# An FFT and two gated layers on one core: decoding the weights in place a pair ahead, with other first turns

## The chip, the cores and the metric

The kernel runs on one NeuronCore of a Trainium2 chip. The metric is the device time of one execution in microseconds. Before the change it is 1013.66 us, the median of three runs (1013.66 to 1013.98).

## What is computed

The input `x` is (2, 3008, 256) in float32. The reference takes the real part of its two-dimensional FFT over sequence and feature, and passes the 6016 rows through two layers whose weights are given in float64:

```python
X = np.fft.fft(np.fft.fft(x, axis=1), axis=2).real.astype(np.float32)
h = X @ w_in                       # 256 -> 2048
X = (h * sigmoid(h)) @ w_out       # 2048 -> 256
h = X @ w_in2
out = (h * np.clip(h + 3, 0, 6) / 6) @ w_out2
```

## The kernel before

**FFT.** `step1`, `step2` and `step3` are three stages of small matmuls; the first comes in 11 chunks of x (`XCH`), the others in 12 steps `g` (`steps23`). `evacuate` copies the result of `step3` from PSUM into `eo`. The symmetry of the transform lets layer one work on 3010 pairs of rows, in six `CHUNKS` of 502 (the last has 500).

**Units.** Each layer is cut into units `(k, f)`: `k` is a turn (`segs`: a chunk and a range of `f`), `f` a block of 128 (layer one) or 256 (layer two) of the 2048 hidden features. Layer one has 96 units in 12 turns: each chunk has a first turn of `PARTS[j]` blocks and, after all six, a second turn with the rest. So the last weights are needed late. Layer two has 96 units as well; its first four turns take blocks 0 to 3, the next four blocks 4 to 7.

A product in float32 accuracy is three matmuls (`mm3`): both operands are split into a rounded part (`hi`) and the rest (`lo`). A unit of layer one runs on PE as `win1` (6 matmuls into `ab`), on DVE as three instructions that make `h`, on ACT as two Silu activations (`parts`, into `ghi` and in place), on POOL as the subtraction `glo` (`low`), and three units later (`LAG`) as `wout1` (12 matmuls into `y`). `ab` and `h` have two buffers each, so `win1` of a unit waits for the `h` of the unit two before it, and that `h` for the `glo` two before. At a turn's end `y` is copied (first turn, ACT) or added (second turn, DVE, L555) to `y1`.

**Weights.** They lie in HBM as pairs of 32-bit words, in eight pairs of blocks per layer. A pair `g` goes through `load_raw` (1 MB by SP's queue), `magnitude` (ACT, L98), five instructions of `bits_to_float32` (DVE, L104 to L116), the additions of `finish_w1` (DVE, L168 to L174), or of `finish_w2`, and `divide`: `whi` on ACT (L161), then `wlo` on DVE (L163). `decoder` is a generator that yields a cost after each DVE instruction; `advance` runs it for a credit in ns, and a PAUSE ends the turn of `advance`. `spare` gives the credit, once per unit in layer one. `win1` drives the generator on where a unit's weights are not yet issued. Four pairs of layer two (`STAGED`) are decoded in layer one's second turns, stored to HBM, and loaded and split shortly before layer two; the other four are decoded in layer two.

**Order.** The program's order is the order on each engine (a manual schedule): nothing is reordered later. The first two units (`EARLY`) are issued at g = 12 and 13, behind the last steps of the FFT.

Of the kernel before, what the change touches and what calls it, by code (L numbers as in the profile page):

```python
# [36 lines left out]
F32 = mybir.dt.float32  # L37
F32R = mybir.dt.float32r
# [21 lines left out]
XCH += [(1, 0, 3), (1, 3, 4), (1, 7, 4), (1, 11, 4), (1, 15, 2)]  # L60
QA = NA + 1

PARTS = (4, 4, 6, 8, 10, 12)
TURNS = 4
LAG = 3
EARLY = 2
# [4 lines left out]
def body(tc, xh, x128, t1, t2, t3, w1, w128, w2, out):  # L71
    nc = tc.nc
    V, A, T, G = nc.vector, nc.scalar, nc.tensor, nc.gpsimd
    per = tc.alloc_tile_pool(name="per", bufs=1)
    wp = tc.alloc_tile_pool(name="wp", bufs=8)
    dp = tc.alloc_tile_pool(name="dp", bufs=1)
    dr = tc.alloc_tile_pool(name="dr", bufs=1, space=bass.MemoryType.DRAM)
    eop = tc.alloc_tile_pool(name="eop", bufs=1, side="right")

# [7 lines left out]

    whi, wlo, raws = {}, {}, {}

    def load_raw(key, src, g, pool=dp):  # L90
        raws[key, g] = pool.tile([P, 2, 512, 2], U32, name=f"raw_{key}_{g}", tag="raw")
        nc.sync.dma_start(raws[key, g], src[:, 2 * g : 2 * g + 2, :, :])


# [2 lines left out]
    def magnitude(raw, t):  # L97
        A.activation(t, raw[..., 1].bitcast(F32), AF.Abs)  # L98

    def bits_to_float32(raw, t, a):  # L100

        high, ai, ti = raw[..., 1].bitcast(I32), a.bitcast(I32), t.bitcast(I32)

        V.tensor_scalar(out=t, in0=t, scalar1=2.0**-15, scalar2=None, op0=ALU.max)  # L104
        yield 680
        V.tensor_scalar(
            out=ai, in0=ti, scalar1=3, scalar2=0x3FFFFFFF, op0=ALU.logical_shift_left, op1=ALU.bitwise_and
        )
        yield 680
        V.scalar_tensor_tensor(  # L110
            out=ai, in0=high, scalar=-0x40000000, in1=ai, op0=ALU.bitwise_and, op1=ALU.bitwise_or
        )
        yield 1200
        V.tensor_scalar(out=ti, in0=ai, scalar1=-0x800000, scalar2=None, op0=ALU.bitwise_and)
        yield 680
        V.scalar_tensor_tensor(out=t, in0=raw[..., 0], scalar=2.0**-52, in1=t, op0=ALU.mult, op1=ALU.mult)  # L116
        yield 1200

    def decoder(key, src, finish, first=0, end=NF // 2, pools=()):

        for g in range(first, end):
            if g >= first + len(pools):
                load_raw(key, src, g)
                yield PAUSE
            a = dp.tile([P, 2, 512], F32, name="da", tag="da")
            raw = raws.pop((key, g))
            if g < first + len(pools):
                if g == first:
                    ts = [q.tile([P, 2, 512], F32, name="dt", tag="dt") for q in pools]
                    magnitude(raw, ts[0])  # L130
                    yield PAUSE
                t = ts[g - first]
            else:
                t = dp.tile([P, 2, 512], F32, name="dt", tag="dt")
                magnitude(raw, t)
                yield PAUSE
            yield from bits_to_float32(raw, t, a)
            if g + 1 < first + len(pools):
                magnitude(raws[key, g + 1], ts[g + 1 - first])
            yield from finish(g, t, a)  # L140
# [12 lines left out]
    def weight_tiles(key, g):
        whi[key, g] = wp.tile([P, 2, 512], F32R, name=f"whi{key}_{g}", tag="whi")
        wlo[key, g] = wp.tile([P, 2, 512], F32R, name=f"wlo{key}_{g}", tag="wlo")

    finished = []

    def divide(key, g, t):
        hi, lo = whi[key, g], wlo[key, g]  # L160
        A.activation(hi, t, AF.Copy)  # L161
        yield PAUSE
        finished.extend([V.tensor_tensor(out=lo, in0=t, in1=hi, op=ALU.subtract)] * 2)  # L163
        yield 1200

    def finish_w1(g, t, a):
        weight_tiles(1, g)
        V.tensor_tensor(out=a[:, :, 0:256], in0=a[:, :, 0:256], in1=t[:, :, 0:256], op=ALU.add)  # L168
        yield 680
        V.tensor_tensor(out=t[:, :, 256:512], in0=a[:, :, 256:512], in1=t[:, :, 256:512], op=ALU.add)  # L170
        yield 680
        V.tensor_tensor(out=t[:, :, 0:128], in0=a[:, :, 0:128], in1=a[:, :, 128:256], op=ALU.add)
        yield 420
        V.scalar_tensor_tensor(  # L174
            out=t[:, :, 128:256], in0=a[:, :, 0:128], scalar=mask, in1=a[:, :, 128:256],
            op0=ALU.mult, op1=ALU.subtract,
        )
        yield 420
        yield from divide(1, g, t)

    def finish_w2(g, t, a):
        weight_tiles(2, g)
        V.tensor_tensor(out=t, in0=a, in1=t, op=ALU.add)
        yield 1200
        yield from divide(2, g, t)

    def store_w2(g, t, a):
        V.tensor_tensor(out=t, in0=a, in1=t, op=ALU.add)
        nc.sync.dma_start(w2_d[g], t)
        yield 1200  # L190

    def load_w2(g):
        raws[g] = dp.tile([P, 2, 512], F32, name=f"w2_{g}", tag="raw")
# [4 lines left out]
        split(whi[2, g], wlo[2, g], raws.pop(g))  # L198

    def decode_w128(raw):  # L200
        t, a = (dp.tile([P, NF], F32, name=n, tag=n) for n in ("w128t", "w128a"))
        magnitude(raw, t)
        yield PAUSE
        for _ in bits_to_float32(raw, t, a):
            yield 70
        V.tensor_tensor(out=w128_sb, in0=a, in1=t, op=ALU.add)
        yield 70
# [144 lines left out]
    steps = itertools.chain(
        decode_w128(w128_raw), decoder(1, w1, finish_w1, pools=(fft, dp)), decoder(2, w2, store_w2, 0, STAGED)
    )
    steps2 = decoder(2, w2, finish_w2, STAGED)
# [5 lines left out]
    def step1_next():  # L361

        nonlocal folded, i
        x = folded
        if i + 4 < nx:
            load_x(i + 4)
        if i + 1 < nx:
            folded = fold(i + 1)
        step1(i, x)
        i += 1  # L370
        if i == 1:
            nc.sync.dma_start(t2_sb, t2)
            nc.sync.dma_start(t3_sb, t3)
            nc.sync.dma_start(w128_raw, w128)
        if i < 5:
            busy(3)
        if i == 5:
            step1_last()
        if i == nx - 4:
            load_raw(1, w1, 0, fft)  # L380
            load_raw(1, w1, 1)
            advance(steps, 1)
        if i == nx - 3:
            advance(steps, 400)

    def steps23(g):
        nonlocal done
        if g < 12:
            o2[g] = step2(g)
        if 0 <= g - 1 < 12:  # L390
            full[g - 1] = step3(o2.pop(g - 1))
        if 0 <= g - 2 < 12:
            done = evacuate(g - 2, full.pop(g - 2))

    while XCH[i][0] == 0:
        step1_next()
    while i < nx:
        steps23(g)
        g += 1
        step1_next()  # L400
        do_later()
        if i >= nx - 1:
            advance(steps, 2500 if i < nx else 1500)
    xp.release()
    psX.release()

# [74 lines left out]
    ]  # L481
    while g < 14:
        steps23(g)
        if g >= 12:
            k, f = units[g - 12]
            gs[k, f] = win1(k, f)
            parts(k, f)
        do_later()
        if g == 8:
            xs[0] = split_eo(0)  # L490
        advance(steps, 1300)
# [95 lines left out]
    for i in range(len(units) + LAG):  # L587
        if i < len(units):
            k, f = units[i]
            layer, j, fs = segs[k]  # L590
            
            if i >= EARLY:
                gs[k, f] = (win1 if layer == 1 else win2)(k, f)
        if 1 <= i <= len(units):
            low(*units[i - 1])
        if i >= LAG:
            k_, f_ = units[i - LAG]
            (wout1 if segs[k_][0] == 1 else wout2)(k_, f_)
# [12 lines left out]
        if 2 <= i < turn:
            spare()
        elif i < n1:

            if i == turn:
                for _ in steps:
                    pass
                load_w2(0)
            g, odd = divmod(i - turn, 2)
            if odd and 0 < g < STAGED:  # L620
                load_w2(g)
            elif not odd and 0 < g <= STAGED:
# [138 lines left out]
```

## Time and profile before

| | |
|---|---|
| median of three runs | 1013.66 us |
| profiled execution | 1013.63 us, span 1011.8 us |
| PE busy | 974.9 us (96%) |
| DVE / ACT / POOL busy | 664.5 (66%) / 513.0 (51%) / 237.5 us (23%) |
| mean granted clock | 0.988 |

The span runs from the first to the last instruction. Busy shares are means over stages: POOL works in layer one alone, and DVE decodes the weights there. A row of a timeline gives start, duration, engine, line, operation and tiles, and in brackets how long the engine had been idle and what released it.

### The profile page before, as it was taken

To read this page: it belongs to the slowest core of one execution; us is meant where nothing else is said; L and a number is where in the kernel's file an instruction comes from. 1 tells how busy PE (TensorE), PEld (TensorE's weight loads), DVE (VectorE), ACT (ScalarE), POOL (GpSimd) and SP (SyncE) were. 2 spreads that over 40 slices of the span, in tenths; PEclk is the share of its full clock that TensorE was granted. 3 is DMA by queue.
4 is the path that set the end of the run, shared out by engine and by line. 5 is a ranking of instruction groups with operands and counts; after the bars stand their busy time and mean duration, and the time that the engine had idled before them with its cause. 6 is when DMAs were issued, how large, how long until landed. Compare 5 with 4: busy or idle time off the path is not lost.

```text
span 1011.8 us, 10957 instructions
## 1 busy us (share of the span) xinstructions
PE 974.9 (96%) x4416; PEld 807.4 (80%) x4416; DVE 664.5 (66%) x724; ACT 513.0 (51%) x559; POOL 237.5 (23%) x101
## 2 busy tenths in 40 slices
PE   8959899999998999999999899999999999999998
PEld 7847678887777888888888688888888888888886
DVE  6769788889997888786777654554534444444443
ACT  3745566565555555565555444443444434344342
POOL 0025556565556565555000000000000000000000
PEclk9979899999999999999999999999999999999999
DMA  9311011011102111021111000000000000000000
GB/s 364 119 52 52 11 42 53 0 52 53 42 1 72 63 54 47 25 74 42 42 41 42 1 21 21 21 20 1 21 21 1 21 1 21 0 21 21 1 21 20
DMA packets 11007, 40.46 MB, mean 40 GB/s; under 512 B 1350, under 2 KB 6348, under 8 KB 8140
## 3 DMA queue, kind: packets, MB, share of 16 engines
q1 hardware_dynamic: 10812, 39.49, 10.9%
q8 instruction: 34, 0.56, 0.2%
q10 hardware_dynamic: 144, 0.27, 0.1%
q14 instruction: 17, 0.14, 0.0%
HBM read 31.48 MB, written 8.27 MB: 39 GB/s over the span
## 4 chain that ended last, share of the span: by engine, by line
PE 81%; DVE 10%; ACT 3%; issue 3%; POOL 1%; DMA 1%; ACTq 0%; POOLq 0%; DVEq 0%
PE y L231 15%; PE y L232 15%; PE y L233 15%; PE ab L233 12%; PE ab L231 12%; PE ab L232 12%; DVE h L461 2%; DVE h L464 2%; POOL glo L531 1%; DMA x<-in_xh 1%; DVE h L465 1%; DVE wlo L163 1%; DVE dt L104 1%; ACT h L475 1%; PE ps L281 1%
## 5 line engine op out<-in xcount | busy, mean ns | idle before, releaser
L231 PE MATMUL y<-ghi,whi 128*128 128x502 f32 (+1 forms) x768 | 301.1, 392 | 2.7 <-DVE y L555 2.7
L233 PE MATMUL y<-ghi,wlo 128*128 128x502 f32 (+1 forms) x768 | 300.8, 392 | 0.0
L232 PE MATMUL y<-glo,whi 128*128 128x502 f32 (+1 forms) x768 | 300.3, 391 | 0.0
L531 POOL TENSOR_TENSOR glo<-h,ghi 128x1004 fp32r<-128x1004 f32 (+1 forms) x96 | 237.1, 2471 | 237.3 <-ACT h L475 209.6
L521 DVE SCALAR_TENSOR_TENSOR h<-h,ab 128x1004 f32<-128x1004 f32 (+1 forms) x96 | 115.2, 1200 | 258.6 <-ACT h L520 258.4
L520 ACT ACTIVATE h<-ab,three 128x1004 f32<-128x1004 f32 (+1 forms) x96 | 105.5, 1099 | 159.5 <-PE ab L233 143.9
L474 ACT ACTIVATE ghi<-h 128x1004 fp32r<-128x1004 f32 (+1 forms) x96 | 100.1, 1043 | 164.3 <-DVE h L465 159.9
L231 PEld LDWEIGHTS y<-ghi,whi 128*128 128x128 f32 x768 | 145.4, 189 | 33.8 <-issue 3.1
L232 PEld LDWEIGHTS y<-glo,whi 128*128 128x128 f32 x768 | 145.9, 190 | 30.9
L233 PEld LDWEIGHTS y<-ghi,wlo 128*128 128x128 f32 x768 | 145.2, 189 | 30.4
L472 ACT ACTIVATE ghi<-h 128x1004 fp32r<-128x1004 f32 (+1 forms) x96 | 100.3, 1045 | 122.0 <-DVE h L521 122.0
L233 PE MATMUL ab<-uhi,wlo 128*128 128x502 f32 (+1 forms) x384 | 150.6, 392 | 3.7 <-DVE wlo L163 3.7
L231 PE MATMUL ab<-uhi,whi 128*128 128x502 f32 (+1 forms) x384 | 150.3, 391 | 0.0
L232 PE MATMUL ab<-ulo,whi 128*128 128x502 f32 (+1 forms) x384 | 150.1, 391 | 0.0
L531 DVE TENSOR_TENSOR glo<-h,ghi 128x1004 fp32r<-128x1004 f32 (+1 forms) x96 | 114.9, 1197 | 0.0
L461 DVE SCALAR_TENSOR_TENSOR h<-eb,w_sb,ab 128x502 f32<-128x502 f32 (+1 forms) x96 | 70.3, 732 | 52.6 <-PE ab L233 39.3
L475 ACT ACTIVATE h<-h 128x1004 f32<-128x1004 f32 (+1 forms) x96 | 100.2, 1044 | 8.7
L231 PE MATMUL ab<-xhi,whi 128*128 128x502 f32 (+1 forms) x192 | 76.5, 398 | 16.9 <-ACT whi L161 12.7
L233 PEld LDWEIGHTS ab<-uhi,wlo 128*128 128x128 f32 x384 | 72.6, 189 | 19.2 <-DVE wlo L163 4.1
L232 PEld LDWEIGHTS ab<-ulo,whi 128*128 128x128 f32 x384 | 72.8, 190 | 15.3
L231 PEld LDWEIGHTS ab<-uhi,whi 128*128 128x128 f32 x384 | 72.7, 189 | 15.2
L233 PE MATMUL ab<-xhi,wlo 128*128 128x502 f32 (+1 forms) x192 | 76.5, 398 | 3.0 <-DVE wlo L163 2.9
(76 smaller groups left out, 800.0 us busy)
## 6 DMA issues: line engine op xcount, KB each, us to landing
raw<-in_w SPq DMA_DIRECT2D x16, 1024.0 KB, 4.8
x<-in_xh SPq DMA_DIRECT2D x6, 1024.0 KB, 6.8
out<-y SPq DMA_DIRECT2D x20, 251.0 KB, 2.2
eb<-e_d SPq DMA_DIRECT2D x10, 251.0 KB, 3.3
w_d<-dt SPq DMA_DIRECT2D x4, 512.0 KB
w<-w_d SPq DMA_DIRECT2D x4, 512.0 KB, 3.2
x<-in_xh SPq DMA_DIRECT2D x3, 512.0 KB
out<-y SPq DMA_DIRECT2D x4, 250.0 KB, 2.0
```

The lines of the kernel that those rows point to most:

```text
L104: V.tensor_scalar(out=t, in0=t, scalar1=2.0**-15, scalar2=None, op0=ALU.max)
L231: T.matmul(o, wh, xhi, start=first, stop=False)
L232: T.matmul(o, wh, xlo, start=False, stop=False)
L233: T.matmul(o, wl, xhi, start=False, stop=last)
L461: V.scalar_tensor_tensor(out=h[:, 0, :n], in0=eb[:, :n], scalar=w128_sb[:, f : f + 1], in1=ab[:, 0, :n], op0=ALU.mult, op1=ALU.add)
L464: V.tensor_tensor(out=h[:, 1, :n], in0=h[:, 0, :n], in1=ab[:, 1, :n], op=ALU.subtract)
L472: A.activation(ghi[:, :, :n], h[:, :, :n], AF.Copy)
L474: A.activation(ghi[:, :, :n], h[:, :, :n], AF.Silu)
L475: A.activation(h[:, :, :n], h[:, :, :n], AF.Silu)
L520: A.activation(h[:, :, :n], hp[:, :, :n], AF.Relu, bias=three)
L521: V.scalar_tensor_tensor(out=h[:, :, :n], in0=h[:, :, :n], scalar=6.0, in1=hp[:, :, :n], op0=ALU.min, op1=ALU.mult)
L531: eng.tensor_tensor(out=glo[:, :, :n], in0=h[:, :, :n], in1=ghi[:, :, :n], op=ALU.subtract)
```

## The change

It does six things. The first turns are of 2, 4, 4, 6, 8 and 10 units. Each pair's decoding uses as scratch the place in which the next pair's weights will lie (`begin`, `scratch`; pools `wp` with a tag per pair); the scratch tiles' room becomes a second buffer for raw words (`dp` with two). `load_raw` runs two pairs ahead and the magnitude one pair ahead of the DVE work. `whi` is issued at a pair's end, and `wlo` (`last_step`) after the second instruction of the next pair. The first two units are issued at g = 11 and 12, inside the FFT, and `xs[0]` and `xs[1]` at g = 7 and 10; `evacuate` goes ahead of `step2`. `spare` gives 1150 per unit (1500 for the first four), and the pairs staged for layer two have a generator of their own (`stage`).

```diff
-PARTS = (4, 4, 6, 8, 10, 12)
+PARTS = (2, 4, 4, 6, 8, 10)
...
-    wp = tc.alloc_tile_pool(name="wp", bufs=8)
-    dp = tc.alloc_tile_pool(name="dp", bufs=1)
+    wp = tc.alloc_tile_pool(name="wp", bufs=1)
+    dp = tc.alloc_tile_pool(name="dp", bufs=2)
...
+    def begin(key, g):
+        if g + 1 < NF // 2:
+            scratch[g] = [wp.tile([P, 2, 512], F32, name=f"{n}{key}_{g}", tag=f"w{n}{g + 1}") for n in ("hi", "lo")]
+        else:
+            both = dp.tile([P, 2, 2, 512], F32, name=f"ta{key}", tag="raw")
+            scratch[g] = [both[:, 0], both[:, 1]]
+        magnitude(raws[key, g], scratch[g][1])
+
+    def decoder(key, src, add, first=0, end=NF // 2):
+        def last_step(g):
+            t = scratch.pop(g)[1]
+            finished.extend([V.tensor_tensor(out=wlo[key, g], in0=t, in1=whi[key, g], op=ALU.subtract)] * 2)
 
         for g in range(first, end):
...
+            (a, t), raw = scratch[g], raws.pop((key, g))
+            for n, cost in enumerate(bits_to_float32(raw, t, a)):
+                yield cost
+                if n == 1 and g > first:
+                    last_step(g - 1)
+                    yield 1200
+            if g + 2 < end:
+                load_raw(key, src, g + 2)
+            if g + 1 < end:
+                begin(key, g + 1)
+            yield from add(t, a)
+            weight_tiles(key, g)
+            A.activation(whi[key, g], t, AF.Copy)
+        yield PAUSE
+        last_step(end - 1)
+        yield 1200
...
+        if i + 4 == nx - 1:
+            load_raw(1, w1, 0)
...
     def steps23(g):
         nonlocal done
+        if 0 <= g - 2 < 12:
+            done = evacuate(g - 2, full.pop(g - 2))
         if g < 12:
             o2[g] = step2(g)
         if 0 <= g - 1 < 12:
             full[g - 1] = step3(o2.pop(g - 1))
-        if 0 <= g - 2 < 12:
-            done = evacuate(g - 2, full.pop(g - 2))
...
-            advance(steps, 1200 if i < 54 else 900)
+            advance(steps, 1500 if i < 4 else 1150)
...
-        if g >= 12:
-            k, f = units[g - 12]
+        do_later()
+        if g in (7, 10):
+            xs[g // 10] = split_eo(g // 10)
+        if g >= 11 and g - 11 < EARLY:
+            k, f = units[g - 11]
             gs[k, f] = win1(k, f)
             parts(k, f)
...
-            elif g > STAGED and i >= n1 - 2:
-                advance(steps2, 1)
+            elif g > STAGED:
+                if i == n1 - 4:
+                    load_raw(2, w2, STAGED)
+                    load_raw(2, w2, STAGED + 1)
+                elif i == n1 - 1:
+                    begin(2, STAGED)
```

In the orders below, `whi1_1` is layer 1, pair 1; `dt` and `da` (before) and `lo` and `hi` (after) are the scratch tiles; the h rows are three to a unit.

On DVE, from the `h` of unit 1 before the change on:

```order
L465 TENSOR_TENSOR h_567<-h_567,ab_566 128x502
L168 TENSOR_TENSOR da_511<-da_511,dt_380 128x2x256
L170 TENSOR_TENSOR dt_380<-da_511,dt_380 128x2x256
L172 TENSOR_TENSOR dt_380<-da_511 128x2x128
L174 SCALAR_TENSOR_TENSOR dt_380<-da_511,mask_73 128x2x128
L163 TENSOR_TENSOR wlo1_1_581<-dt_380,whi1_1_580 128x1024
L461 SCALAR_TENSOR_TENSOR h_606<-eb0_488,w128_sb_71,ab_605 128x502
```

and from the last decode instruction of the same pair after it, ahead of the `h` of unit 2:

```order
L180 SCALAR_TENSOR_TENSOR lo1_1_474<-hi1_1_473,mask_73 128x2x128
L471 SCALAR_TENSOR_TENSOR h_610<-eb1_532,w128_sb_71,ab_609 128x502
L474 TENSOR_TENSOR h_610<-h_610,ab_609 128x502
L475 TENSOR_TENSOR h_610<-h_610,ab_609 128x502
L104 TENSOR_SCALAR lo1_2_591<-lo1_2_591 128x1024
L106 TENSOR_SCALAR hi1_2_590<-lo1_2_591 128x1024
L471 SCALAR_TENSOR_TENSOR h_631<-eb1_532,w128_sb_71,ab_630 128x502
L474 TENSOR_TENSOR h_631<-h_631,ab_630 128x502
L475 TENSOR_TENSOR h_631<-h_631,ab_630 128x502
L142 TENSOR_TENSOR wlo1_1_626<-lo1_1_474,whi1_1_625 128x1024
L110 SCALAR_TENSOR_TENSOR hi1_2_590<-raw_1_2_471,hi1_2_590 128x1024
```

`wlo1_1` stood ahead of the `h` of unit 2; now the `h` of units 2 and 3 and the first two instructions of pair 2 stand ahead of it.

On DVE at the start of pair 6, before the change behind the `h` of unit 37:

```order
L104 TENSOR_SCALAR dt_1721<-dt_1721 128x1024
L106 TENSOR_SCALAR da_1720<-dt_1721 128x1024
L110 SCALAR_TENSOR_TENSOR da_1720<-raw_1_6_1690,da_1720 128x1024
L461 SCALAR_TENSOR_TENSOR h_1760<-eb5_1405,w128_sb_71,ab_1759 128x500
```

and after it behind the `h` of unit 28:

```order
L104 TENSOR_SCALAR lo1_6_1431<-lo1_6_1431 128x1024
L471 SCALAR_TENSOR_TENSOR h_1507<-eb5_1204,w128_sb_71,ab_1506 128x500
L474 TENSOR_TENSOR h_1507<-h_1507,ab_1506 128x500
L475 TENSOR_TENSOR h_1507<-h_1507,ab_1506 128x500
L167 TENSOR_TENSOR xlo0_1496<-eo_74,xhi0_1495 128x1004
L106 TENSOR_SCALAR hi1_6_1430<-lo1_6_1431 128x1024
L471 SCALAR_TENSOR_TENSOR h_1537<-eb5_1204,w128_sb_71,ab_1536 128x500
L474 TENSOR_TENSOR h_1537<-h_1537,ab_1536 128x500
L475 TENSOR_TENSOR h_1537<-h_1537,ab_1536 128x500
L142 TENSOR_TENSOR wlo1_5_1503<-lo1_5_1241,whi1_5_1502 128x1024
```

Three instructions of a pair stood in a row between two `h`s; now they are spread over three units, with the previous pair's `wlo` between.

On DVE in layer two, the end of the last pair, before the change (L521 is a unit's `h`, L531 its `glo`):

```order
L183 TENSOR_TENSOR dt_4126<-da_4125,dt_4126 128x1024
L521 SCALAR_TENSOR_TENSOR h_4239<-h_4239,ab_4238 128x1004
L531 TENSOR_TENSOR glo_4255<-h_4200,ghi_4201 128x1004
L147 TENSOR_TENSOR ulo1_4236<-y1_592,uhi1_4235 128x1004
L163 TENSOR_TENSOR wlo2_7_4232<-dt_4126,whi2_7_4231 128x1024
L521 SCALAR_TENSOR_TENSOR h_4275<-h_4275,ab_4274 128x1004
```

and after it (L531 and L541):

```order
L187 TENSOR_TENSOR ta2_3941<-ta2_3941 128x1024
L531 SCALAR_TENSOR_TENSOR h_4059<-h_4059,ab_4058 128x1004
L541 TENSOR_TENSOR glo_4075<-h_4026,ghi_4027 128x1004
L531 SCALAR_TENSOR_TENSOR h_4097<-h_4097,ab_4096 128x1004
L541 TENSOR_TENSOR glo_4113<-h_4059,ghi_4060 128x1004
L167 TENSOR_TENSOR ulo0_4094<-y1_606,uhi0_4093 128x1004
L142 TENSOR_TENSOR wlo2_7_4091<-ta2_3941,whi2_7_4090 128x1024
L531 SCALAR_TENSOR_TENSOR h_4133<-h_4133,ab_4132 128x1004
```

`wlo2_7` stood ahead of the `h` of that layer's unit 19 (counted from 0); now it stands ahead of unit 15's.

## Rows read from the trace of the kernel before

**Rows 1.** Timeline of PE: matmuls at and behind its holes.
```profile
51.20 1.16 PE L325 MATMUL ps<-t_sb,o 128*128 128x128 f32 x8 [1.04 <-ACT eo L339]
...
65.61 0.79 PE L231 MATMUL ab<-xhi,whi 128*128 128x502 f32 x1 [10.50 <-ACT whi L161]
...
74.32 0.39 PE L231 MATMUL y<-ghi,whi 128*128 128x502 f32 x1
74.55 0.39 PE L232 MATMUL y<-glo,whi 128*128 128x502 f32 x1
...
109.27 0.50 PE L231 MATMUL ab<-xhi,whi 128*128 128x502 f32 x1 [2.17 <-ACT whi L161]
...
111.99 0.79 PE L233 MATMUL ab<-xhi,wlo 128*128 128x502 f32 x1 [1.99 <-DVE wlo L163]
...
116.75 0.42 PE L232 MATMUL y<-glo,whi 128*128 128x502 f32 x1
...
148.21 0.49 PE L233 MATMUL ab<-xhi,wlo 128*128 128x502 f32 x1 [0.93 <-DVE wlo L163]
...
231.33 0.50 PE L231 MATMUL ab<-xhi,whi 128*128 128x500 f32 x1 [1.08 <-DVE h L465]
...
265.92 0.49 PE L231 MATMUL ab<-xhi,whi 128*128 128x502 f32 x1 [1.53 <-DVE h L465]
...
300.72 0.49 PE L231 MATMUL ab<-xhi,whi 128*128 128x502 f32 x1 [1.67 <-DVE h L465]
...
317.36 0.47 PE L231 MATMUL y<-ghi,whi 128*128 128x502 f32 x1 [2.73 <-DVE y L555]
...
577.84 0.79 PE L233 MATMUL ab<-uhi,wlo 128*128 128x502 f32 x1 [3.66 <-DVE wlo L163]
...
580.93 0.43 PE L231 MATMUL ab<-uhi,whi 128*128 128x502 f32 x1
```

**Rows 2.** Busy time in a stretch: length, PE, PEld, DVE, ACT, POOL, clock.
```profile
120.00:140.00 20.00, 20.00 (x89) 16.56 (x88) 18.80 (x24) 12.37 (x14) 10.61 (x5) 1.00 0.21 65
```

**Rows 3.** Timeline of DVE: decoding of pair 0, `h` of unit 0, end of pair 1.
```profile
34.29 0.69 DVE L104 TENSOR_SCALAR dt<-dt 128x1024 f32<-128x1024 f32 x1 [3.03 <-ACT dt L98]
...
37.01 0.69 DVE L114 TENSOR_SCALAR dt<-da 128x1024 int32<-128x1024 int32 x1
...
39.61 0.68 DVE L170 TENSOR_TENSOR dt<-da,dt 128x512 f32<-128x512 f32 x1
...
53.77 0.74 DVE L461 SCALAR_TENSOR_TENSOR h<-eb,w_sb,ab 128x502 f32<-128x502 f32 x1 [3.09 <-PE ab L233]
...
55.85 1.22 DVE L116 SCALAR_TENSOR_TENSOR dt<-raw,dt 128x1024 f32<-128x1024 uint32 x1
...
65.59 1.23 DVE L163 TENSOR_TENSOR wlo<-dt,whi 128x1024 fp32r<-128x1024 f32 x1 [1.12 <-ACT whi L161]
```

**Rows 4.** Timeline of ACT: the two activations of unit 0.
```profile
55.97 1.04 ACT L474 ACTIVATE ghi<-h 128x1004 fp32r<-128x1004 f32 x1 [4.25 <-DVE h L465]
57.04 1.04 ACT L475 ACTIVATE h<-h 128x1004 f32<-128x1004 f32 x1
```

**Rows 5.** Timelines of POOL and DVE: a `glo` beside a decode addition.
```profile
61.37 2.42 POOL L531 TENSOR_TENSOR glo<-h,ghi 128x1004 fp32r<-128x1004 f32 x1 [0.89 <-ACT h L475]
...
61.55 2.52 DVE L172 TENSOR_TENSOR dt<-da 128x256 f32<-128x256 f32 x1
```

**Rows 6.** Waits: engine, waited for, us in total, times, longest.
```profile
PE ps L325 <- ACT eo L339: 2.4, 4, 1.0
...
ACT dt L98 <- DMA raw<-in_w: 0.4, 1, 0.4
```

**Rows 7.** Timeline of DVE: start of pair 7.
```profile
257.78 1.93 DVE L104 TENSOR_SCALAR dt<-dt 128x1024 f32<-128x1024 f32 x1 [0.96 <-ACT dt L98]
...
260.48 3.31 DVE L110 SCALAR_TENSOR_TENSOR da<-raw,da 128x1024 int32<-128x1024 int32 x1
263.71 0.72 DVE L461 SCALAR_TENSOR_TENSOR h<-eb,w_sb,ab 128x502 f32<-128x502 f32 x1
```

More of the change, by code (lines that the diff above doesn't have):

```diff
@@ L88, in body, with load_raw @@
     whi, wlo, raws = {}, {}, {}
-    def load_raw(key, src, g, pool=dp):
-        raws[key, g] = pool.tile([P, 2, 512, 2], U32, name=f"raw_{key}_{g}", tag="raw")
+    def load_raw(key, src, g):
+        raws[key, g] = dp.tile([P, 2, 512, 2], U32, name=f"raw_{key}_{g}", tag="raw")
         nc.sync.dma_start(raws[key, g], src[:, 2 * g : 2 * g + 2, :, :])
@@ L117, in bits_to_float32 @@
         yield 1200
-    def decoder(key, src, finish, first=0, end=NF // 2, pools=()):
-        for g in range(first, end):
[L122 to L140, printed above, removed]
+    finished = []
@@ new lines, in weight_tiles @@
+    def weight_tiles(key, g):
+        whi[key, g] = wp.tile([P, 2, 512], F32R, name=f"whi{key}_{g}", tag=f"whi{g}")
+        wlo[key, g] = wp.tile([P, 2, 512], F32R, name=f"wlo{key}_{g}", tag=f"wlo{g}")
+    scratch = {}
+    def begin(key, g):
[5 more added lines that the diff above has]
+        magnitude(raws[key, g], scratch[g][1])
@@ L151, in do_later, with add_w1 @@
             later.pop(0)()
[L153 to L167, printed above, removed]
+    def add_w1(t, a):
         V.tensor_tensor(out=a[:, :, 0:256], in0=a[:, :, 0:256], in1=t[:, :, 0:256], op=ALU.add)
@@ L178, in finish_w1, with add_w2, stage @@
         yield 420
-        yield from divide(1, g, t)
-    def finish_w2(g, t, a):
-        weight_tiles(2, g)
+    def add_w2(t, a):
         V.tensor_tensor(out=t, in0=a, in1=t, op=ALU.add)
         yield 1200
[L185 to L190, printed above, removed]
+    def stage():
+        for g in range(STAGED):
+            load_raw(2, w2, g)
+            yield PAUSE
+            ta = dp.tile([P, 2, 2, 512], F32, name=f"ta{g}", tag="raw")
+            t, a, raw = ta[:, 0], ta[:, 1], raws.pop((2, g))
+            magnitude(raw, t)
+            yield PAUSE
+            yield from bits_to_float32(raw, t, a)
+            V.tensor_tensor(out=t, in0=a, in1=t, op=ALU.add)
+            nc.sync.dma_start(w2_d[g], t)
+            yield 1200
     def load_w2(g):
@@ L200, in decode_w128 @@
     def decode_w128(raw):
-        t, a = (dp.tile([P, NF], F32, name=n, tag=n) for n in ("w128t", "w128a"))
+        t, a = (fft.tile([P, NF], F32, name=n) for n in ("w128t", "w128a"))
         magnitude(raw, t)
@@ L351, in body @@
     nc.sync.dma_start(xl, x128)
[L352 to L355, printed above, removed]
+    steps = itertools.chain(decode_w128(w128_raw), decoder(1, w1, add_w1), stage())
+    steps2 = decoder(2, w2, add_w2, STAGED)
     o2, full, done = {}, {}, 0
@@ L379, in step1_next @@
         if i == nx - 4:
-            load_raw(1, w1, 0, fft)
             load_raw(1, w1, 1)
             advance(steps, 1)
-        if i == nx - 3:
-            advance(steps, 400)
     def steps23(g):
         nonlocal done
+        if 0 <= g - 2 < 12:
+            done = evacuate(g - 2, full.pop(g - 2))
         if g < 12:
@@ L400, in body @@
         step1_next()
-        do_later()
-        if i >= nx - 1:
-            advance(steps, 2500 if i < nx else 1500)
+        if i == nx - 1:
+            begin(1, 0)
+            advance(steps, 400)
+    advance(steps, 800)
     xp.release()
@@ L483, in body @@
         steps23(g)
-        if g >= 12:
-            k, f = units[g - 12]
+        do_later()
[3 more added lines that the diff above has]
+            k, f = units[g - 11]
             gs[k, f] = win1(k, f)
             parts(k, f)
[L488 to L491, printed above, removed]
+        advance(steps, 1700 if g < 8 else 1400)
         g += 1
@@ L607, in body @@
             spare()
-        if f == fs[len(fs) // 2 - 1] and k + 1 < len(segs):
+        if f == fs[len(fs) // 2 - 1] and k + 1 < len(segs) and k + 1 not in xs:
             l_, j_, _ = segs[k + 1]
```

## The prediction

> **What bounds the kernel now.** I read the engines' busy shares first (PE is at 96%, so the time is PE's matmuls plus the holes in them), then PE's timeline for the holes, then the list of waits and the timelines of VectorE (DVE), ScalarE (ACT) and GpSimd (POOL) in front of each hole. In the timeline of PE [rows 1] two successive matmuls without a wait start 0.23 us apart (74.32 to 74.55). A first-layer unit is 18 of them, 6 into `ab` (win1) and 12 into `y` (wout1): 18 x 0.2275 = 4.1 us. The same rows show the holes, and what released them: 10.50 us before unit 2, which needs the second pair of weights, 2.17 and 1.99 before unit 12 (third pair), 0.93 at unit 20 (fourth pair), 1.08, 1.53 and 1.67 behind VectorE's `h`, 2.73 behind its accumulation of `y`, and 3.66 in layer two at the last pair. After a long hole the matmuls come at the lower of TensorE's two clock levels: from 111.99 to 116.75 there are eleven starts, 0.43 us apart, so that hole costs 4.76 - 11 x 0.2275 = 2.3 us beyond its own length; from 577.84 to 580.93 seven starts cost 3.09 - 1.6 = 1.5 us more.
>
> So PE waits for decoded weights, and those are VectorE's work. In the stretch 120 to 140 [rows 2] PE is busy 20.00 of 20 us beside a VectorE busy 18.80: the decode's mean rate can be carried, and it is its dates that miss.
>
> **VectorE's prices.** One `h` (three instructions) runs from 53.77 to 55.85: 2.08 us [rows 3]. The first seven decode instructions run from 34.29 to about 40.2: 5.9 us, of which the first three are 2.7; the two short ones after them I put at 0.75, and the subtraction that ends a pair is 1.23. Between a ready `h` and POOL's `glo` lie two activations, 55.97 to 58.08 [rows 4]. POOL's `glo` holds VectorE up: one began at 61.37 and took 2.42, and a decode addition that began at 61.55 took 2.52, ending when POOL's had ended and 0.2 us had passed [rows 5].
>
> The Trainium skill says why, in "SBUF — State Buffer", section "Who interferes with whom": a VectorE instruction with two SBUF inputs and a GpSimd one that reads SBUF exclude each other, and the one that issues first keeps the port to its end. Rows 5 agree. By that rule a decode that is cut into more places between the `h`s has more chances of coming second, which speaks against this change; what that would give is the second rival below.
>
> **The change, term by term** (gain in us, against the profiled execution, 1013.63, which is 0.03 below the median of the three runs).
>
> *Start.* Now units 0 and 1 stand inside the FFT, and units 0 to 3 need only pair 0. When pair 1 is whole, PE will have done the `ab` matmuls of units 2 and 3 and the `y` matmuls of unit 0 besides: 24 x 0.2275 = 5.5 us of work that stood behind the hole. When is it whole? Before at 65.59 + 1.23 = 66.8 [rows 3]. After: the four waits of step 3 for an evacuation, 2.4 us in all [rows 6], should go, since evacuations now stand first on ACT, and the last step 3 (at 51.20 [rows 1]; 0.9 of its 1.16, the rest being the modelled end) stands behind unit 0; so the first `h` starts near 53.77 - 3.3 = 50.5. Behind it on VectorE stand, until pair 1 is whole: four `h`s, 8.3; the rest of pair 1's decode, 3.0 + 0.75 + 1.23; the first two of pair 2, 1.3; and two waits for POOL, 0.75 and 1.2. That is 16.5, so 67.0, about as before. But the last decode instruction of pair 1 meets POOL's second `glo` within 0.1 us by this walk. If POOL is first, 2.4 us are added: 69.4. The nearest row (61.37 against 61.55) has POOL first, so I take 5.5 - 2.4 + 0.1 = **3.2**; ends 3.2 and 5.5. A hole of some 6 to 8 us stays, now in front of unit 4.
>
> *Pairs 2 and 3.* In VectorE's order the third pair's last step now stands ahead of unit 10's `h` and is due at unit 14, the fourth's ahead of unit 17's and due at unit 22; before they stood at 12 and 20, the unit that needs them. Four units are 16 us of cover. 2.17 + 1.99 + 2.3 + 0.93 = **7.4**. If VectorE falls behind by a unit or more, part of it stays; lower end 4.
>
> *Starts of pairs 6 and 7.* Before, three decode instructions in a row follow ACT's magnitude, and POOL catches two of them: L104 at 257.78 (with 0.96 idle for ACT), L110 at 260.48 lasting 3.31, `h` only at 263.71 [rows 7], and PE waits at 231.33 and 265.92 [rows 1]. Now the magnitude is issued a pair earlier and at most two of these stand between two `h`s. **2.6**; ends 0 and 2.6.
>
> *Staged pairs of the second layer.* Their code keeps the run of three (before units 46, 52, 58 and 64). Before, the first of four cost 1.67, and the accumulation of `y` after it 2.73. I count **0**: the same is paid again, earlier. Ends: +4.4 (+1.5 with the lower clock), and -5.0 if three more runs cost 1.67 each, since they now stand unbroken where `spare` gave less per unit before.
>
> *Layer two.* The last pair's final step now stands ahead of the `h` of that layer's unit 15 instead of unit 19, where it is due. 3.66 + 1.5 = **5.2**; no row gives a reason for a lower end but a late transfer, and these are now issued four units before layer two.
>
> *Transfers a pair ahead*: ACT waited for a raw pair once, 0.4 us [rows 6]: **0**, its cover being the buffer's early issue. Moving the second buffer into the place of the scratch tiles costs nothing while the places' old users are done; they are, by unit order. In the input stage pair 0's transfer passes one last half-size chunk of x in SP's queue; PE is busy with the chunks before, and I put this at 0 too.
>
> Sum 3.2 + 7.4 + 2.6 + 0 + 5.2 = 18.4, so **995.2 us**.
>
> **Rivals.** (1) *The run of three is paid four times and the pair starts still stall*: 3.2 + 7.4 + 0 - 5.0 + 5.2 = 10.8, giving 1002.8; beyond it if pairs 2 and 3 come late as well. For it: three holes of this make in 70 us of the old trace. Against: of the ten pair starts from the third pair to the last staged one only those three show one. (2) *VectorE becomes the bound, slower than before.* Place: units 4 to 46, where the decode now runs without a pause. Per unit 2.08 for `h`, some 1.06 of decode (1150 of credit), 0.2 for splits; a full POOL wait (2.1) in every unit makes 5.4 against PE's 4.1, 42 x 1.3 = 55 us of loss: 1050. It decides the sign once the mean POOL wait is above 4.1 - 3.34 + 18.4 / 42 = 1.2 us. Against: rows 2, the same rate with no hole. (3) *VectorE wins the close meeting and the staging is smooth*: 5.5 + 7.4 + 2.6 + 5.9 + 5.2 = 26.6, giving 987. (4) *The transfers are the point, and they were hidden*: nothing moves, 1013.6; the order of the instructions speaks against it.
>
> **How the numbers follow.** A measurement of this kernel tells 0.2% (2 us) from no change. Forecast with rival 3, 986 to 1002.5: 0.80; below 986: 0.03; rival 1 from 1002.5 to 1011.6: 0.10; rival 4: 0.02; rival 2: 0.05. Faster 0.93, same 0.02, slower 0.05. The range 986 to 1002.5 runs from rival 3 (and 1 us for an earlier first `h`) to rival 1.
>
> **What would show it.** Right: one hole of 6 to 8 us before unit 4, near 60 to 69, with `wlo` as releaser; none at units 14 and 22; no wait of PE for `wlo` in layer two; holes of 1 to 3 us only behind starts of staged pairs and a `y` accumulation. Wrong: PE waiting for VectorE's `h` every few units between 100 and 240, or a wait for `wlo` at units 44 to 46.

## The result and the profile after

The changed kernel takes **990.35 us** (median of four runs, 989.55 to 991.16); the kernel before, beside it on the same chip, 1013.82. The ratio is 0.9763, 95% interval 0.9746 to 0.978. Forecast were 995.2 in a range of 986 to 1002.5. The profiled execution took 989.55 us, span 987.7, clock 0.995.

The busy row of the page, and two stretches of its table by windows (length, PE, PEld, DVE, ACT, POOL, clock, DMA share, GB/s):

```profile
PE 972.2 (98%) x4416; PEld 807.9 (82%) x4416; DVE 657.7 (67%) x724; ACT 512.3 (52%) x559; POOL 234.8 (24%) x101
```

```profile
60.00:63.90 3.90, 3.90 (x10) 3.12 (x11) 3.76 (x7) 3.04 (x3) 1.72 (x2) 0.50 0.16 49
...
120.00:140.00 20.00, 18.41 (x80) 14.61 (x79) 19.66 (x20) 12.23 (x15) 11.49 (x5) 1.00 0.03 6
```

PE is busy 2.7 us less than before, mostly because fewer matmuls run at the lower clock; the other 21 us are idle time that went. In 120 to 140, where PE had no hole [rows 2], it now has one (the 1.37 us at 125.22 below), and VectorE is busy 19.66 of the 20 us.

These are the holes in PE's timeline, to be held against [rows 1]. Units 3, 4, 5, 18 and 48 start at 56.21, 64.67, 70.29, 125.22 and 251.87:

```profile
56.21 0.49 PE L243 MATMUL ab<-xhi,whi 128*128 128x502 f32 x1 [2.29 <-DVE h L475]
...
59.96 0.79 PE L243 MATMUL y<-ghi,whi 128*128 128x502 f32 x1 [1.73 <-ACT eo L351]
...
63.47 0.62 PE L245 MATMUL y<-ghi,wlo 128*128 128x502 f32 x1
63.89 0.48 PE L243 MATMUL y<-ghi,whi 128*128 128x502 f32 x1
...
66.51 0.49 PE L245 MATMUL ab<-xhi,wlo 128*128 128x502 f32 x1 [1.22 <-DVE wlo L142]
...
70.29 0.39 PE L243 MATMUL ab<-xhi,whi 128*128 128x502 f32 x1
...
125.22 0.50 PE L243 MATMUL ab<-xhi,whi 128*128 128x502 f32 x1 [1.37 <-DVE h L475]
...
251.87 0.79 PE L243 MATMUL ab<-xhi,whi 128*128 128x502 f32 x1 [2.57 <-DVE h L475]
...
255.32 0.39 PE L245 MATMUL y<-ghi,wlo 128*128 128x502 f32 x1
```

The 10.50 us before unit 2 are gone, and so are the holes at the third, fourth, sixth and seventh pair and the one in layer two. What is left at the start is three short waits in series, for `h`, for an evacuation of the FFT and for `wlo`. Behind the second, ten matmuls come 0.42 us apart at a granted clock of 0.50, the lower level.

### The profile page after: what moved, and what is told of

Same layout as the page of the kernel before. It is cut to its first block, busy times and chain, and to the rows that moved or that the text cites. A ratio compares the mean times of both kernels' runs of the same rounds, so it can differ in the third digit from the quotient of the medians.

```text
span 987.7 us, 10943 instructions
## 1 busy us (share of the span) xinstructions
PE 972.2 (98%) x4416; PEld 807.9 (82%) x4416; DVE 657.7 (67%) x724; ACT 512.3 (52%) x559; POOL 234.8 (24%) x101
## 4 chain that ended last, share of the span: by engine, by line
PE 81%; DVE 13%; issue 3%; ACT 2%; DMA 1%; ACTq 0%; DVEq 0%
PE y L243 14%; PE y L245 14%; PE y L244 14%; PE ab L243 12%; PE ab L245 12%; PE ab L244 12%; DVE h L471 2%; DVE h L474 2%; DVE h L475 2%; DMA x<-in_xh 1%; PE ps L337 1%; PE ps L293 1%; DVE lo L176 1%; DVE wlo L142 1%; DVE lo L116 1%
## 5 line engine op out<-in xcount | busy, mean ns | idle before, releaser
L541 POOL TENSOR_TENSOR glo<-h,ghi 128x1004 fp32r<-128x1004 f32 (+1 forms) x96 | 234.4, 2442 | 219.9 <-ACT h L485 191.5
L531 DVE SCALAR_TENSOR_TENSOR h<-h,ab 128x1004 f32<-128x1004 f32 (+1 forms) x96 | 115.2, 1200 | 255.4 <-ACT h L530 255.4
L541 DVE TENSOR_TENSOR glo<-h,ghi 128x1004 fp32r<-128x1004 f32 (+1 forms) x96 | 114.9, 1197 | 0.0
```

The source lines that it names most:

```text
L531: V.scalar_tensor_tensor(out=h[:, :, :n], in0=h[:, :, :n], scalar=6.0, in1=hp[:, :, :n], op0=ALU.min, op1=ALU.mult)
L541: eng.tensor_tensor(out=glo[:, :, :n], in0=h[:, :, :n], in1=ghi[:, :, :n], op=ALU.subtract)
```

## The experiments

Every run's total is read against the changed kernel's 990.35, its trace against the trace above. Two runs (2 and 7) start from the kernel before, which took 1013.91 beside them. The kernel before, executed again beside each group of runs, took between 1011.0 and 1016.2 us, so a total that is off by less than some 2 us is read from the trace alone.

**1. The first turns alone, put back.**

```diff
-PARTS = (2, 4, 4, 6, 8, 10)
+PARTS = (4, 4, 6, 8, 10, 12)
```

> The changed kernel with the first turns of before (4, 4, 6, 8, 10, 12). The hole then lies in front of unit 2 again, and the h of units 2 and 3 no longer stand ahead of wlo of pair 1. Theory (the turns buy PE work ahead of the hole, and the queue of h before wlo eats most of it): pair 1 is whole 4 to 5 us earlier than the 66.4 of the change, PE has 24 matmuls (5.5 us) less behind it, so 1 to 2 us slower than the change, 991 to 993. Rival (the turns carry the start's whole gain): 5.5 to 7 us slower, 996 to 997.5.

Measured: 996.3 us, 5.95 slower. PE's timeline, at units 2 and 5 and in a second turn:

```profile
61.02 0.79 PE L243 MATMUL ab<-xhi,whi 128*128 128x502 f32 x1 [8.61 <-ACT whi L157]
...
74.94 0.39 PE L243 MATMUL ab<-xhi,whi 128*128 128x502 f32 x1
...
304.68 0.76 PE L243 MATMUL y<-ghi,whi 128*128 128x502 f32 x1 [3.85 <-DVE y L565]
```

Unit 2 needs pair 1 again, and the one long hole is back; unit 5 is 4.65 us late. So most of the start's gain is the turn of two units. The total agrees with that only by chance: at unit 58 no more than 0.46 of the 4.65 us is left, since the first staged pair meets no hole here, and 6.4 us come at unit 60, where the start of a staged pair stands directly ahead of the addition of `y`.

The trace also settles pairs 2 and 3. With these turns they are due at units 12 and 20, as in the kernel before, and no hole is there: units 12 and 20 take 4.11 and 4.09 us, where the kernel before took 8.66 and 5.29. The new decode alone is in time for the old dates.

**2. The same turns in the kernel before.**

```diff
-PARTS = (4, 4, 6, 8, 10, 12)
+PARTS = (2, 4, 4, 6, 8, 10)
```

> The kernel before with the new first turns alone (2, 4, 4, 6, 8, 10). Theory (the turns move the first hole behind four units and give pairs 2 and 3 two units of cover, but call pairs 6 and 7 ten units earlier, where the old decoder is not ready): 5 to 7 us gained at the start, 6 to 7 at pairs 2 and 3, but pair 7 is decoded in one run ahead of unit 46 and PE waits 8 to 15 us there: 1006 to 1014. Rival (the turns do the work, the place and lead of the decode little): 1000 or less.

Measured: 1030.77 us, 16.9 slower than before and far outside what was expected; unit 5 already is 3.7 us late, where 5 to 7 us of gain were expected. PE's timeline:

```profile
63.92 0.79 PE L231 MATMUL ab<-xhi,whi 128*128 128x502 f32 x1 [7.16 <-ACT xhi L146]
...
255.25 0.79 PE L231 MATMUL ab<-xhi,whi 128*128 128x502 f32 x1 [5.03 <-ACT whi L161]
...
277.59 0.79 PE L231 MATMUL ab<-xhi,whi 128*128 128x502 f32 x1 [9.29 <-ACT whi L161]
```

The second chunk's `xhi` isn't ready for unit 2, and the last two pairs, due at units 44 and 46, aren't decoded (pair 7 was due at 54). At units 14 and 22, where pairs 2 and 3 are due here, there is no hole, so the later dates alone end the wait for these weights too; but 3.8 us go at units 16 and 17, behind three decode instructions in a row (L104, L106 and L110 from 121.71). The same table of turns is worth 6 us with the rest of the change, and costs 17 without.

**3. Units 0 and 1 behind the FFT again.**

```diff
-        if g >= 11 and g - 11 < EARLY:
-            k, f = units[g - 11]
+        if g >= 12:
+            k, f = units[g - 12]
```

> The changed kernel with units 0 and 1 issued at g = 12 and 13, behind the FFT's last step 3, as before. Theory (their place inside the FFT moves the first h forward by one step 3): first h 0.9 to 1.5 us later than 50.06, wlo of pair 1 as much later, 991.3 to 992 (up to 994 if the last decode instruction of pair 1 then comes behind POOL's second glo). Rival (their place is what makes the start's gain): 3.5 us slower or more, above 994.

Measured: 992.1 us, 1.75 slower; in the trace unit 0 is 1.3 late, pair 1 is whole 0.72 late, and unit 5 2.96 late. PE's timeline at the second half of unit 4 and at unit 5:

```profile
67.23 0.79 PE L245 MATMUL ab<-xhi,wlo 128*128 128x502 f32 x1 [1.81 <-DVE wlo L142]
...
73.25 0.39 PE L243 MATMUL ab<-xhi,whi 128*128 128x502 f32 x1
```

These 16 matmuls take 6.02 us, in the changed kernel 3.78 (66.51 to 70.29). 2.24 of the 2.96 are thus the lower clock: the slow matmuls lie behind the last wait here, and ahead of it in the changed kernel.

**4. The meeting with POOL.** Six memsets of a scratch tile delay the last operation of pair 1. In the first trial they stood ahead of the additions:

```diff
+            if (key, g) == (1, 1):
+                for _ in range(6):
+                    V.memset(idle, 0.0)
             yield from add(t, a)
```

> The changed kernel with six one-element memsets (each some 0.06 us) put on VectorE between the h of unit 1 and the additions of pair 1, so that the last decode instruction of that pair, which began at 58.19 with POOL's second glo at 58.38, now comes behind the start of that glo. Theory (whichever of the two engines starts first holds the other off): the short delay turns into a full glo, wlo of pair 1 and unit 5's first matmul come 2.3 to 2.8 us later, and the time is 992 to 993.5 against 990.4. Rival (no such exclusion, only the order of VectorE counts): 0.4 us later, 990.7.

Measured: 992.79 us, but it doesn't answer the question. The first addition had been held by POOL's first `glo` (L174 takes 1.25 us at 56.08 in the changed kernel, 0.69 here), so the memsets fell into a wait that was there anyway, and pair 1 was whole only 0.15 us later. The second trial put them behind the third addition:

```diff
-            yield from add(t, a)
+            for n, cost in enumerate(add(t, a)):
+                yield cost
+                if (key, g, n) == (1, 1, 2):
+                    for _ in range(6):
+                        V.memset(idle, 0.0)
```

> The changed kernel with six short memsets of a scratch tile on VectorE between the third and the last addition of pair 1's second group, so that the first instruction of that group's last operation (L180) stands some 0.5 us later and POOL's second glo begins ahead of it. Theory (the prediction's price of the meeting was right in size and only its order was chosen wrong): L180's first instruction starts at the end of POOL's glo, pair 1 is whole 2.3 to 2.8 us later (the last wlo at about 68.9 where it stands at 66.5), unit 5 starts later by as much or by up to 1.5 us more where a lower clock follows; total 992 to 995. Rival (the two share the time without loss): pair 1 whole some 0.5 us later only, total 989.5 to 990.5.

Measured: 996.46 us in its one execution. VectorE and PE in it (POOL's `glo` ran from 58.52 for 2.31):

```profile
58.94 2.17 DVE L185 SCALAR_TENSOR_TENSOR lo<-hi,mask 128x256 f32<-128x256 f32 x1
```

```profile
68.94 0.79 PE L250 MATMUL ab<-xhi,wlo 128*128 128x502 f32 x1 [1.82 <-DVE wlo L143]
...
74.10 0.39 PE L248 MATMUL ab<-xhi,whi 128*128 128x502 f32 x1
```

Started 0.75 us later than in the changed kernel (58.94 against 58.19), the operation takes 2.17 us where it took 0.48, pair 1 is whole 2.43 us later and unit 5 starts 3.81 us later. The theory's size is right; the total is 2.3 us more than that. The traces say where: in layer two, units 25 to 95 take 384.45 us here and 384.44 in the first trial, and 382.6 in each of the other twelve traces of this document, with no hole in that stretch in any of them. Both edits touch pair 1 alone and the first one left everything else in place, so this longer interval between matmuls belongs to the execution and not to the edit. Layer two as a whole is 2.4 us longer by it in both traces, which is most of what the first trial lost. What lengthens the interval isn't shown; the granted clock of 620 to 960 us reads 1.00 in all fourteen.

**5. Transfers and magnitudes.** First the raw transfer one pair ahead instead of two:

```diff
             (a, t), raw = scratch[g], raws.pop((key, g))
+            if first < g < end - 1:
+                load_raw(key, src, g + 1)
...
-            if g + 2 < end:
-                load_raw(key, src, g + 2)
```

> The changed kernel with each raw pair's transfer issued at the start of the pair before it instead of the end of that pair's bit decoding one earlier (about 16 us of lead instead of 28). Theory (the transfers had cover before and have it now; the lead is not where the time came from): no instruction moves on the compute engines, within 1 us of the change, 989.5 to 991.5. Rival (the lead is what keeps ACT's magnitude from waiting): 2 us slower or more.

Measured: 989.44 us, and no unit starts more than 0.22 us off: the second pair of lead is worth nothing, as forecast. Then the magnitude at the pair's own start:

```diff
             (a, t), raw = scratch[g], raws.pop((key, g))
+            if g > first:
+                begin(key, g)
+                yield PAUSE
...
-            if g + 1 < end:
-                begin(key, g + 1)
...
-            advance(steps, 1500 if i < 4 else 1150)
+            advance(steps, 1500 if i < 4 else 1250)
```

> The changed kernel with each pair's magnitude issued at that pair's own start with a PAUSE behind it, as before, and 1250 of credit in place of 1150 so that the last pair is still done by unit 43. Theory (the magnitude a pair ahead removes VectorE's wait for ACT at a pair's start and lets its instructions spread, worth the 2.6 us of pairs 6 and 7): holes behind h at two or more pair starts between units 16 and 40, 992.5 to 995. Rival (the holes come from VectorE's load alone): 989.5 to 991.5.

Measured: 997.42 us, but elsewhere than expected. PE's timeline:

```profile
68.85 0.64 PE L246 MATMUL ab<-xhi,wlo 128*128 128x502 f32 x1 [2.66 <-DVE wlo L142]
...
303.55 0.49 PE L244 MATMUL ab<-xhi,whi 128*128 128x502 f32 x1 [2.29 <-DVE h L476]
```

VectorE waits 1.51 us for the magnitude of pair 2 ahead of pair 1's `wlo`, and unit 5 is 3.9 us late; at unit 44 the delay is still 3.6. So at the pair starts in between the early magnitude was worth nothing (the edit's 100 ns more of credit per unit may have helped). At pair 7 VectorE waits for ACT again (0.90 us ahead of L104 at 206.16), but an `h` still parts L106 from L110, and PE has no hole there. The rest of the loss comes at the staged pairs, which the edit only shifts.

**6. The staged pairs.** In the changed kernel VectorE's and POOL's timelines at the first of them read:

```profile
243.73 1.96 DVE L104 TENSOR_SCALAR ta<-ta 128x1024 f32<-128x1024 f32 x1 [0.96 <-ACT ta L98]
...
246.45 3.29 DVE L110 SCALAR_TENSOR_TENSOR ta<-raw,ta 128x1024 int32<-128x1024 int32 x1
249.67 0.73 DVE L471 SCALAR_TENSOR_TENSOR h<-eb,w_sb,ab 128x502 f32<-128x502 f32 x1
```

```profile
242.75 2.39 POOL L541 TENSOR_TENSOR glo<-h,ghi 128x1004 fp32r<-128x1004 f32 x1 [2.18 <-ACT h L485]
245.84 2.82 POOL L541 TENSOR_TENSOR glo<-h,ghi 128x1004 fp32r<-128x1004 f32 x1 [0.70 <-ACT h L485]
```

Two `glo`s close together hold up one decode instruction each, as in [rows 7]: L104 1.96 instead of 0.69, L110 3.29 instead of some 1.2. The edit cuts the run of instructions:

```diff
-            yield from bits_to_float32(raw, t, a)
+            for n, cost in enumerate(bits_to_float32(raw, t, a)):
+                yield cost
+                if n == 1:
+                    yield PAUSE
```

> The changed kernel with a PAUSE after the second of the decode instructions of each pair staged for layer two, so that no run of three stands between two h. Theory (the run of three, caught twice by POOL, made the hole of 2.57 us at 251.87 and the lower clock behind it): that hole goes or falls below 1 us, 986 to 988. Rival (VectorE is late there from the pairs before, and the hole only moves on to the next h or to the accumulation of y): 989.5 to 991.

Measured: 989.54 us. The hole at 251.87 is gone, unit 54 is 3.3 us early, and unit 74 is where it was (360.53 against 360.52), because PE's timeline has new ones:

```profile
264.00 0.46 PE L246 MATMUL y<-ghi,whi 128*128 128x502 f32 x1 [1.10 <-DVE y L568]
...
305.29 0.50 PE L246 MATMUL ab<-xhi,whi 128*128 128x502 f32 x1 [1.05 <-DVE h L478]
...
316.19 0.46 PE L246 MATMUL y<-ghi,whi 128*128 128x502 f32 x1 [1.08 <-DVE y L568]
```

The rival was right: VectorE was late, not only badly cut. Then the same cut with less work per unit, so that the four staged pairs end in unit 75 instead of 67:

```diff
-            advance(steps, 1500 if i < 4 else 1150)
+            advance(steps, 1500 if i < 4 else 1150 if i < 46 else 800)
```

> The changed kernel with VectorE's decode run of the staged pairs cut by a pause, as in the run that split it, and with 800 credits instead of 1150 at the starts of the stages from unit 46 on, so that less decode work stands ahead of each FFT's h. Theory (VectorE is late only because the decode work comes in lumps at the stage starts): the hole of 2.57 us at 252 is gone and isn't moved on, unit 74 starts 2.5 to 4.5 us earlier; total 985 to 987. Rival (VectorE has no slack left between units 46 and 78, so a later decode gives a hole further on): unit 74 within 1 us of the changed kernel's; total 989 to 991.

Measured: **986.62 us**, ratio to before 0.9729 (0.9698 to 0.976). Unit 74 starts 2.9 us early; of the holes behind unit 46 one is left, 1.50 behind the addition of `y` at 264.42. So VectorE has room there, once the work isn't dense. Less work per unit without the cut was not run.

**7. Layer two, in the kernel before.**

```diff
-            advance(steps2, 2000)
+            advance(steps2, 2800)
```

> The kernel before with 2800 instead of 2000 of credit per unit for the decode inside layer two, nothing else: its last pair then stands ahead of the h of layer two's unit 16 instead of 19. Theory (the hole of 3.66 us and the lower clock behind it are that pair's date alone): 5.2 us faster than before, 1008 to 1009. Rival (moving decode work earlier in layer two makes PE wait for h or y there): 1010 or more.

Measured: 1007.81 us (three runs, 1004.62 to 1008.97). The hole at 577.84 [rows 1] is gone. That layer's unit 24 starts 5.84 us earlier than before, its unit 0 already 0.49: the step itself is worth 5.35, and it was one late step.

**8. The start in another order.** The FFT's last evacuation goes ahead of unit 1's activations on ACT, pair 1's `whi` directly behind its last addition, and the first four units get more credit:

```diff
+        if g == 12:
+            done = evacuate(11, full.pop(11))
         if g >= 11 and g - 11 < EARLY:
...
             A.activation(whi[key, g], t, AF.Copy)
+            yield 420 if key == 1 else 1200
...
-            advance(steps, 1500 if i < 4 else 1150)
+            advance(steps, 1900 if i < 4 else 1150)
```

> The changed kernel with three edits of the start: the FFT's last evacuation is placed ahead of unit 1's activations, pair 1's high parts are copied directly behind its last addition, ahead of the next unit's ghi on ScalarE, and the credit of the first four units is 1900 instead of 1500, so that the last low part of pair 1 stands ahead of unit 3's h. Theory (the three waits in series at 56, 60 and 66 are orders of instructions, not work): the holes of 1.73 us at 59.96 and 1.22 us at 66.51 shrink to under 0.5 us each and unit 5 starts 2 to 4 us earlier; total 985.5 to 988. Rival (VectorE and POOL are full there and each wait only stands in front of the next): unit 5 within 1 us of the changed kernel's; total 989 to 991.

Measured: 990.1 us. Unit 5 starts 2.06 us early, as expected, and the total doesn't show it. PE's and ACT's timelines at unit 9:

```profile
88.42 0.50 PE L243 MATMUL y<-ghi,whi 128*128 128x502 f32 x1 [1.61 <-ACT y L565]
```

```profile
85.92 1.03 ACT L167 ACTIVATE xhi<-eo 128x1004 fp32r<-128x1004 f32 x1
86.85 1.04 ACT L157 ACTIVATE whi<-lo 128x1024 fp32r<-128x1024 f32 x1
87.80 2.01 ACT L565 ACTIVATE y<-y 128x502 f32<-128x502 f32 x4
```

The edit also moved the next pair's `whi` ahead of the evacuation of `y`, and PE waits for that. Unit 46 is still 1.93 us early; at the staged pairs, reached with a longer lead of the decode, holes of 1.31 and 2.27 us took the rest.

**9. Both together**, with the early `whi` for pair 1 alone and a credit of 1700:

```diff
+            for n, cost in enumerate(add(t, a)):
+                if (key, g, n) == (1, 1, 3):
+                    weight_tiles(key, g)
+                    A.activation(whi[key, g], t, AF.Copy)
+                yield cost
+            if (key, g) != (1, 1):
+                weight_tiles(key, g)
+                A.activation(whi[key, g], t, AF.Copy)
...
-            advance(steps, 1500 if i < 4 else 1150)
+            advance(steps, 1700 if i < 4 else 1150 if i < 46 else 800)
```

> The changed kernel with the slower, split runs of the staged pairs (800 credits from unit 46 on, a pause behind the second decode instruction) and with the start of the run that put the last evacuation of the FFT and pair 1 first, but with the early copy of the high parts for pair 1 alone and 1700 credits instead of 1900 in the first four units, so that the later pairs keep the changed kernel's places. Theory (the two gains are of different stretches and add, as the start's 2.0 us were lost again by the copies of the later pairs, which stood ahead of an evacuation of y at unit 9, and by the longer lead at the staged pairs): unit 5 about 2 us before the changed kernel's, no hole over 0.5 us at unit 9 or at 252; total 984 to 985.5. Rival (a lead at the start is only idle time that VectorE needs, and comes back as a hole further on): unit 46 within 0.7 us of the changed kernel's, total 986 to 987.

Measured: **981.64 us** (five runs, 981.44 to 982.8), ratio to before 0.9677 (0.9657 to 0.9697): it beats both kernels, and by 2.4 us the lower end of what was expected. PE's timeline from unit 3 on:

```profile
57.37 0.49 PE L251 MATMUL ab<-xhi,whi 128*128 128x502 f32 x1 [2.29 <-DVE h L483]
...
62.03 0.46 PE L251 MATMUL ab<-xhi,whi 128*128 128x502 f32 x1 [0.30 <-DVE h L483]
...
64.51 0.49 PE L253 MATMUL ab<-xhi,wlo 128*128 128x502 f32 x1 [1.78 <-DVE wlo L142]
...
68.29 0.39 PE L251 MATMUL ab<-xhi,whi 128*128 128x502 f32 x1
...
260.59 0.47 PE L251 MATMUL y<-ghi,whi 128*128 128x502 f32 x1 [1.37 <-DVE y L575]
```

From unit 3 to unit 4 it is 4.66 us where the changed kernel took 8.46 (56.21 to 64.67): the wait for the evacuation and the lower clock behind it are both gone, for 1.2 us of a later start. The hole before unit 18 went too: an `h` (114.13) now parts pair 4's first two instructions (L104 at 113.53, L106 at 116.20), which stood in a row in the changed kernel. That I hadn't counted. Unit 46 is 3.74 us early and unit 74 6.74, of which the staged pairs' 2.9 is the part that the second trial of 6 showed. The rival falls.

## Why the prediction was right

The gains in us, by how much earlier units start than in the trace before. Unit 48 carries the last old hole of pairs 6 and 7 and the first new one of the staged pairs; there the two are told apart by what each unit takes beyond 4.1 us.

| step | forecast | measured |
|---|---|---|
| start | 3.2 | 6.8 |
| pairs 2 and 3 | 7.4 | 7.0 |
| starts of pairs 6 and 7 | 2.6 | 2.95 |
| staged pairs | 0 | 2.0 |
| layer two | 5.2 | 5.35 |
| sum | 18.4 | 24.1 |

**Start.** This is the term that was mis-sized, and the step that failed is "The nearest row (61.37 against 61.55) has POOL first, so I take 5.5 - 2.4 + 0.1". VectorE's and POOL's timelines after:

```profile
50.06 0.74 DVE L471 SCALAR_TENSOR_TENSOR h<-eb,w_sb,ab 128x502 f32<-128x502 f32 x1 [0.63 <-PE ab L245]
...
58.19 0.48 DVE L180 SCALAR_TENSOR_TENSOR lo<-hi,mask 128x256 f32<-128x256 f32 x1
...
64.11 2.34 DVE L142 TENSOR_TENSOR wlo<-lo,whi 128x1024 fp32r<-128x1024 f32 x1
```

```profile
58.38 2.46 POOL L541 TENSOR_TENSOR glo<-h,ghi 128x1004 fp32r<-128x1004 f32 x1 [1.61 <-ACT h L485]
...
63.02 2.35 POOL L541 TENSOR_TENSOR glo<-h,ghi 128x1004 fp32r<-128x1004 f32 x1 [2.18 <-ACT h L485]
```

The first `h` began at 50.06 (forecast 50.5), and VectorE came 0.19 us ahead of POOL, where [rows 5] had it 0.18 behind: the first half of rival 3 came true. Pair 1 was whole at 66.45, against 67.0 in the walk. Run 4 shows the other case: 2.43 us, the 2.4 of the forecast. The price was right and the order wrong. Nothing in the trace before could decide 0.2 us, so the choice was a guess; the range held both outcomes. The Trainium skill ("SBUF — State Buffer", "Who interferes with whom") agrees with both orders: who issues first keeps the port (VectorE's 0.48 us against POOL, 2.17 behind it).

The other part was not in the forecast. PE's timeline before, from pair 1's first low-part matmul to unit 5:

```profile
66.87 0.79 PE L233 MATMUL ab<-xhi,wlo 128*128 128x502 f32 x1
...
77.06 0.39 PE L231 MATMUL ab<-xhi,whi 128*128 128x502 f32 x1
```

Before, these 40 matmuls took 10.19 us, 1.09 over 40 x 0.2275; after, the 16 from 66.51 to 70.29 took 3.78, 0.14 over. So 0.36 (earlier) + 24 x 0.2275 = 5.46 + 0.95 (clock) = 6.8. The lower clock's price at the third pair and in layer two was counted; at the start it was left out.

**Pairs 2 and 3.** The mechanism is as forecast, and by runs 1 and 2 either half of it ends the wait for these weights: the new decode alone at no other cost, the later dates alone with 3.8 us of holes behind `h` in its place. The size agrees in part by luck. The old waits at units 12 and 20 were worth 8.1 us by the units' starts, and 1.0 of a hole at unit 8, not in the sum, went as well; 2.1 came back at units 17 to 19, where the forecast had no hole. Most of that is the hole before unit 18. VectorE's and POOL's timelines ahead of it, at the start of pair 4:

```profile
117.73 2.55 DVE L104 TENSOR_SCALAR lo<-lo 128x1024 f32<-128x1024 f32 x1
120.31 2.79 DVE L106 TENSOR_SCALAR hi<-lo 128x1024 int32<-128x1024 int32 x1
123.02 0.73 DVE L471 SCALAR_TENSOR_TENSOR h<-eb,w_sb,ab 128x502 f32<-128x502 f32 x1
```

```profile
117.36 2.36 POOL L541 TENSOR_TENSOR glo<-h,ghi 128x1004 fp32r<-128x1004 f32 x1 [4.98 <-ACT h L485]
120.16 2.39 POOL L541 TENSOR_TENSOR glo<-h,ghi 128x1004 fp32r<-128x1004 f32 x1 [0.44 <-ACT h L485]
```

Two decode instructions in a row are held by a `glo` each, 2.55 and 2.79 us for 0.69: such a meeting, which rival 2 puts into every unit, held PE up here and not again up to unit 47.

**Pairs 6 and 7.** The size is as forecast (2.6 and 2.95). Of the two reasons given, the magnitude a pair earlier is not the one: run 5 put it back and no hole came at their starts. What is left is the other, that at most two decode instructions stand between two `h`s; no run tried that alone.

**Staged pairs.** Before, the start and the addition cost 6.4 with the clock; after, only the first start, 4.4. So 2.0 us were gained where 0 was counted, inside its ends. That the later three starts cost nothing is a matter of where they fall: with other turns (run 1) a staged pair's start cost 6.4 at unit 60. Runs 6 and 9 show what is left there.

**Layer two and transfers.** As forecast, and shown singly by run 7 and by the first trial of run 5.

**What was to be seen.** One hole of 6 to 8 us was expected before unit 4. It came as 2.29, 1.73 and 1.22 us, with ten slow matmuls behind the second. The 1.73 was missed altogether: the walk went by weights and `h`, and didn't ask who had held the PSUM banks that `y` takes over.

## What to carry to other kernels

Price a late weight by everything that stands between its arrival and the next point that both versions share, the clock level included, and look where slow matmuls lie: ahead of the last wait they cost nothing more here. Where a decode comes in lumps between fixed instructions, cutting its runs alone gained nothing and cutting and spreading them 2.9 us. An edit that moves one copy forward is to be followed on that engine's queue to whatever it now stands in front of. A table of turns that gains 6 us in one version and loses 17 in another is to be judged only together with the dates that it sets.

## What was not expected of the hardware

A hole of 2.29 us alone left the clock up (18 starts in 4.66 us behind 57.37, run 9); the same hole followed 3.75 us later by one of 1.73 was followed by ten starts at the lower level (59.96), and one of 2.57 after a steady stretch by eight (251.87 to 255.32). In run 3 a hole of 2.57 us before the same unit 48 (254.81) left the clock up: that unit took 4.22 us there and 5.75 in the changed kernel. The length of a hole alone doesn't tell what follows it. And a delay of 0.75 us on VectorE became 2.43 us at the weight and 3.81 at unit 5 (run 4), through one meeting with POOL and the clock behind it.
